# The order in which an instruction's waits are issued, in a kernel planned op by op

## The chip, the cores and the metric

The kernel runs on one core of a Trainium2 chip. The metric is the device time of one execution in microseconds (us), lower being better; times of several runs are given as their median. A profile of one execution is read beside them.

## The reference

Four layers follow each other on a sequence of 2048 rows of 512 numbers: A, B, A, B. Each normalizes its input and adds its result to it.

```python
# A: 32 query heads of 16, one key head and one value head for all of them
scores = jnp.einsum("bhqd,bkd->bhqk", q, k) * (Dh ** -0.5)
p = _softmax(scores, axis=-1)
o = jnp.einsum("bhqk,bkd->bhqd", p, v)
# B: linear attention, 32 heads of 16
phi = lambda t: jnp.where(t > 0, t + 1, jnp.exp(t)) + 1e-6
kv = jnp.einsum("bhsd,bhse->bhde", pk, v)
o = num / den
x = x + _A_ref(_layernorm(x, axis=-1), ...)   # then B, A, B
```

## The kernel before

Nothing is looped on the chip. Python code describes the work as operations, a planner in the same file runs them once against its own estimate of time, and the order that comes out on each engine is what is issued. The stretches that fill most of the time are the two A layers. There a group of two or three score blocks (128 keys by 512 columns, four heads by 128 queries) is made by TensorE into two or three PSUM banks (line 807, called from the operation of line 965). ScalarE takes the exponential of the whole group into one of six PT buffers (line 973). TensorE then multiplies PT by V into an accumulation bank (line 861). Beside this, VectorE makes a further block's exponential by integer arithmetic from PSUM into FB (line 1049), adds shifted copies of it (line 1080), and TensorE multiplies those too by weighted V (also line 861). Short matmuls of line 906 fill TensorE where it has nothing else. GpSimd computes the power of each layernorm (line 655). SyncE issues all DMAs (lines 507, 583, 1467).

An operation may be issued when those that it depends on are done: those that wrote what it reads, and those that wrote or read what it overwrites. `Planner.op` collects them in a Python set, `o.deps`. The planner notes for each operation the time at which it is planned to end, `o.end`. When the order of all engines is fixed, `finalize` (lines 274 to 294) gives each operation that others need a place in the count of its engine's semaphore (`s_pe`, `s_act`, `s_dve`, `s_pool`); a DMA gets one of 24 semaphores of its own.

`emit` (lines 296 to 313) then walks one engine's order. For each operation it keeps, of every engine that it depends on, the dependency with the highest count, in a dictionary `need`, whose order is the order in which the set gave them up: that of the objects in memory, not of time. A dependency on the same engine counts too on VectorE, ScalarE and GpSimd; so an exponential of line 973 waits for TensorE (`s_pe`: the scores, or the matmul that read the PT buffer last) and, if that is not covered by an earlier wait, for ScalarE itself (`s_act`: the exponential that wrote the same PT buffer some five exponentials earlier). A score matmul of line 807 waits for ScalarE and VectorE, which read its banks before. For each entry of `need` not already waited for, `eng.wait_ge` is called (line 310), and then the operation is issued.

## Time and profile before

| what | value |
| --- | --- |
| median of 3 runs | 1555.51 us (1555.47 to 1560.37) |
| the profiled execution: time | 1556.79 us |
| the profiled execution: span from first to last instruction | 1555.1 us |
| granted TensorE clock, mean | 0.996 |
| TensorE matmul, ScalarE, VectorE busy | 1458.7, 1476.8, 1448.3 us |
| GpSimd busy | 68.8 us |
| line 973, exponentials on ScalarE | 1361, 1424.5 us busy |
| line 807, score matmuls | 4096 |
| line 861, matmuls by V | 4068 from FB, 3079 from PT |

PE is TensorE's matmul, PEld its loading of weights, ACT ScalarE, DVE VectorE, POOL GpSimd, SP SyncE. A q behind an engine's name (ACTq) means its sequencer: the part that takes the instructions in order and hands them to the engine. In a group's line stand the source line, the engine, the operation, what is written and read with the sizes, how many there are, busy time and mean duration, and the idle time just before them with what ended most of it. The chain of work that ended last is followed back from the last instruction, at each step to what released it, or to the instruction before it on its engine; "issue" in it is time in which an engine waited for nothing that the profile shows.

### The profile page before, as it was taken

How to read it: one execution, taken by the hardware profiler on the slowest of the kernel's cores; microseconds unless marked ns; L12 is line 12 of the kernel's file. 1: busy time of each engine (PE TensorE's matmuls, PEld its weight loads, DVE VectorE, ACT ScalarE, POOL GpSimd, SP SyncE). 2: the span in 40 equal slices, each digit the busy share in tenths (PEclk: the TensorE clock that was granted, in tenths of full speed). 3: DMA queues.
4: the chain of work that ended last, by engine and by line, in shares of the span. 5: the costliest groups of instructions: out<-in, count | busy, mean ns of one | idle time of the engine just before them, and what ended most of it. 6: DMA issues, size and time to landing. Idle time of an engine off the chain costs nothing.

```text
span 1555.1 us, 36056 instructions
## 1 busy us (share of the span) xinstructions
PE 1458.7 (94%) x14602; PEld 535.4 (34%) x14713; DVE 1448.3 (93%) x2707; ACT 1476.8 (95%) x1500; POOL 68.8 (4%) x122
## 2 busy tenths in 40 slices
PE   8998999999999999999999989999999999999999
PEld 4322332333333333333644323323333333333345
DVE  7999999999999999998676799999999999999977
ACT  8999999999999999999699999899999999999982
POOL 4000000000000000000111000000000000000000
PEclk9999999999999999999999999999999999999998
DMA  5100010000000000000000000000000000000001
GB/s 132 47 2 1 8 22 5 8 8 5 8 8 8 5 8 5 1 1 1 2 1 1 1 1 15 15 8 8 6 9 5 8 8 8 5 5 2 1 2 55
DMA packets 40435, 17.55 MB, mean 11 GB/s; under 512 B 34128, under 2 KB 39760, under 8 KB 40272
## 3 DMA queue, kind: packets, MB, share of 16 engines
q1 hardware_dynamic: 40272, 15.25, 4.2%
q8 instruction: 118, 1.93, 0.5%
q14 instruction: 45, 0.37, 0.1%
HBM read 5.28 MB, written 2.10 MB: 5 GB/s over the span
## 4 chain that ended last, share of the span: by engine, by line
PE 32%; issue 23%; DVE 23%; ACT 20%; POOL 1%; DMA 0%; SPq 0%; ACTq 0%; POOLq 0%; DVEq 0%
ACT PT L973 19%; DVE FB L1049 11%; PE ps L861 11%; PE ps L807 9%; DVE FB L1080 6%; PE ps L575 4%; PE ps L906 2%; PE ps L732 2%; PE ps L1122 1%; POOL rs L655 1%; DVE st L651 1%; DVE sacc L1103 1%; PE ps L793 1%; ACT phE L1205 1%; DVE xn L658 1%
## 5 line engine op out<-in xcount | busy, mean ns | idle before, releaser
L973 ACT ACTIVATE PT<-ps 128x1024 bf16<-128x1024 f32 (+1 forms) x1361 | 1424.5, 1180 | 19.9 <-PE ps L861 13.4
L1049 DVE TENSOR_SCALAR FB<-ps 128x512 int16<-128x512 f32 x1017 | 675.0, 686 | 23.5 <-PE ps L807 20.7
L807 PE MATMUL ps<-QT,KM 32*128 32x512 bf16 x4096 | 533.4, 384 | 46.8 <-ACT PT L973 27.9
L861 PE MATMUL ps<-FB,VW 128*32 128x512 bf16 x4068 | 530.4, 385 | 19.5 <-ACT PT L973 9.5
L861 PE MATMUL ps<-PT,V 128*32 128x512 bf16 x3079 | 513.0, 386 | 9.7 <-ACT PT L973 5.6
L1080 DVE TENSOR_SCALAR FB<-FB 128x2048 int16<-128x2048 int16 (+1 forms) x765 | 503.0, 683 | 0.9
L807 PEld LDWEIGHTS ps<-QT,KM 32*128 32x128 bf16 x4096 | 139.8, 91 | 445.3 <-ACT PT L973 203.8
L861 PEld LDWEIGHTS ps<-FB,VW 128*32 128x32 bf16 x4068 | 133.4, 94 | 219.5 <-issue 113.0
L861 PEld LDWEIGHTS ps<-PT,V 128*32 128x32 bf16 x3079 | 125.9, 94 | 111.8 <-issue 56.1
L906 PE MATMUL ps<-QT,V 128*32 128x512 bf16 (+6 forms) x568 | 131.0, 315 | 0.9 <-DVE FB L1049 0.9
L655 POOL TENSOR_TENSOR rs<-ve,mhalf 128x1 f32<-128x1 f32 x64 | 51.7, 811 | 1398.9 <-DVE ve L653 1386.0
L575 PE MATMUL ps<-wqkv,xnT 128*128 128x512 bf16 (+1 forms) x211 | 65.1, 368 | 3.9 <-issue 2.9
L906 PEld LDWEIGHTS ps<-QT,V 128*32 128x32 bf16 x568 | 44.1, 95 | 59.6 <-issue 39.3
L1103 DVE COPY sacc<-ps 128x512 f32<-128x512 f32 x64 | 43.8, 684 | 7.8 <-PE ps L861 7.6
L1205 ACT ACTIVATE phE<-ps 128x512 bf16<-128x512 f32 (+1 forms) x66 | 41.3, 625 | 6.6 <-PE ps L732 4.7
L1122 PE MATMUL ps<-identF,sacc 128*128 128x128 f32 x256 | 45.9, 291 | 1.5 <-DVE sacc L1103 0.8
L732 PE MATMUL ps<-xnT,wqkv 128*128 128x128 bf16 x512 | 44.3, 221 | 0.0
L651 DVE BATCH_NORM_STATS2 st<-x_sb 128x6 f32<-128x512 bf16 x60 | 40.8, 683 | 2.6 <-DMA x_sb<-in_A_x_dram 2.3
L1105 DVE TENSOR_TENSOR sacc<-sacc,ps 128x512 f32<-128x512 f32 x56 | 38.2, 682 | 2.4 <-PE ps L861 2.1
L732 PE MATMUL ps<-xnT,wq 128*128 128x128 bf16 x480 | 38.6, 224 | 0.0
L575 PEld LDWEIGHTS ps<-wqkv,xnT 128*128 128x128 bf16 x272 | 21.8, 97 | 44.9 <-issue 34.2
L732 PEld LDWEIGHTS ps<-xnT,wqkv 128*128 128x128 bf16 x512 | 29.1, 98 | 22.8 <-issue 19.4
(115 smaller groups left out, 671.1 us busy)
## 6 DMA issues: line engine op xcount, KB each, us to landing
out_dram<-x_sb SPq DMA_DIRECT2D x16, 128.0 KB, 1.7
x_sb<-in_A_x_dram SPq DMA_DIRECT2D x3, 512.0 KB, 6.1
wqkv<-in_B_wqkv_dram SPq DMA_DIRECT2D x1, 1536.0 KB, 7.5
xnT<-xn SPq DMA_TRANSPOSE x36, 2.4
x_sb<-in_A_x_dram SPq DMA_DIRECT2D x4, 128.0 KB, 2.2
wq<-in_A_wq_dram SPq DMA_DIRECT2D x1, 512.0 KB, 4.2
wo<-in_A_wo_dram SPq DMA_DIRECT2D x1, 512.0 KB, 4.1
wo<-in_B_wo_dram SPq DMA_DIRECT2D x1, 512.0 KB, 8.5
```

Source lines behind the costliest of these rows:

```text
L575: return e.matmul(dst, lhsT=l, rhs=r, start=(k == 0), stop=(k == len(pairs) - 1))
L655: op({PO: (0.55, lambda e: e.tensor_tensor(out=rs[:, t:t + 1], in0=ve[:, t:t + 1], in1=mhalf[:], op=ALU.pow))}, reads=[("ve", t), "mhalf"] ...
L732: ins = e.matmul(dst[:, g * P:(g + 1) * P], lhsT=lhs(g, k), rhs=rhs(k), start=(k == 0), stop=(k == FT - 1))
L807: return e.matmul(bank(b), lhsT=KM[r, sg.par, kt * P:(kt + 1) * P], rhs=QT[r, sg.t, :], start=True, stop=True)
L861: ins = e.matmul(ps[32 * j:32 * j + 32, ACC * 512:(ACC + 1) * 512], lhsT=V[:, kt, :] if w is None else VW[:, kt, w, :], rhs=ap, start=(k = ...
L906: o = op({PE: (n / 2400.0, lambda e: e.matmul(ps[32 * j:32 * j + 32, b * 512:b * 512 + n], lhsT=V0[:], rhs=QT[:, sg.t, 0:n], start=st, sto ...
L973: ex = op({AC: (0.05 + 0.4267 * n, lambda e, n=n, s_=s_, p_=p_: e.activation(PT[:, p_, 0:n * 512], ps[:, s_ * 512:(s_ + n) * 512], ACTF.Ex ...
L1049: o = op({DV: (0.60, lambda e: e.tensor_scalar(out=dst.bitcast(I16), in0=bank(b), scalar1=VB, scalar2=VLO, op0=ALU.add, op1=ALU.max))}, wr ...
L1080: o = op({en: (du, lambda e, w=w, g_=g_: e.tensor_scalar(out=FB[:, g_, 0:n].bitcast(I16), in0=FB[:, f_, 0:n].bitcast(I16), scalar1=float(w ...
L1103: o = op({DV: (0.6, lambda e, src=src: e.tensor_copy(src, bank(ACC)))}, writes=[B_(ACC), key], prio=0.0, lat=0.15)
L1122: o = op({PE: (0.12, lambda e, c=c: e.transpose(ps[:, b * 512 + c * P:b * 512 + (c + 1) * P], src[:, c * P:(c + 1) * P], identF[:]))}, rea ...
L1205: op({AC: (0.07 + n / 1200.0, lambda e: e.activation(phE[:, i, 0:n], bank(b, n), ACTF.Exp))}, reads=[B_(b)], writes=[("phE", i)], prio=min ...
```

## The change

One line of `emit` changes. The entries of `need` are taken in the order of the planned ends of their operations, the earliest first. What is waited for, how often, and the order of the instructions on each engine stay as they are.

```diff
                 if k not in need or need[k].value < d.value:
                     need[k] = d
-            for k, d in need.items():
+            for k, d in sorted(need.items(), key=lambda x: x[1].end):
                 if waited.get(k, 0) >= d.value:
                     continue
                 waited[k] = d.value
                 eng.wait_ge(d.sem, d.value)
             ins = o.fn(eng)
```

## The prediction

> **What bounds the kernel now.** I read the page first: busy shares and the chain that ended last.

> ```profile
> span 1555.1 us, 36056 instructions
> PE 1458.7 (94%) x14602; PEld 535.4 (34%) x14713; DVE 1448.3 (93%) x2707; ACT 1476.8 (95%) x1500; POOL 68.8 (4%) x122
> ...
> PE 32%; issue 23%; DVE 23%; ACT 20%; POOL 1%; DMA 0%; SPq 0%; ACTq 0%; POOLq 0%; DVEq 0%
> ```

> Three engines are busy for 93 to 95% of the span, and none carries the chain: it changes hands between PE, DVE and ACT all the time. So no engine's throughput alone sets the end, and the delay of a handoff (semaphore counted up, next instruction starts) is paid wherever the chain crosses. Handoffs are all that this change touches.

> Next, the instructions of line 310, which are the waits that stand alone:

> ```profile
> L310 ACTq EVENT_SEMAPHORE  x1175: 17/17/1615, 6.3 to 1549.4; - x196
> L310 PEldq EVENT_SEMAPHORE  x875: 51/51/51, 5.5 to 1538.6; - x175
> L310 DVEq EVENT_SEMAPHORE  x114: 21/21/842, 23.0 to 1549.2; - x114
> L310 SPq EVENT_SEMAPHORE  x77: 17/17/26862, 173.8 to 1554.6; - x77
> L310 POOLq EVENT_SEMAPHORE  x52: 17/17/17, 214.6 to 1513.7; - x52
> ```

> Each is the second wait of a two-wait instruction (of SP, of one with up to four). Most are ACT's and PE's; DVE, at 2707 instructions, has only 114.

> Third, the chain in time order (start us, us, what) at single handoffs. PE to ACT at 1137, then at 775:

> ```profile
> 1137.56 0.35 PE ps L807 x3
> 1137.91 0.02 issue
> 1137.93 0.02 ACTq L310
> 1137.94 0.04 issue
> 1137.99 1.03 ACT PT L973
> ```

> ```profile
> 774.83 0.39 PE ps L807 x2
> 775.22 0.02 issue
> 775.24 0.02 ACT PT L973
> ```

> In the first the wait that ended last (on `s_pe`) stood in the EVENT_SEMAPHORE: 0.08 us pass. In the second the exponential carried it, the separate wait (on `s_act`) having been over long before: 0.02 us. ACT to PE at 180.9 and at 119.7 shows the same pair:

> ```profile
> 179.93 0.93 ACT PT L973
> 180.85 0.14 issue
> 180.99 0.39 PE ps L807 x3
> ```

> ```profile
> 118.55 1.19 ACT PT L973
> 119.74 0.05 issue
> 119.79 0.39 PE ps L807 x3
> ```

> 0.14 us against 0.05 us. So the trace of before holds both forms and prices them.

> **What the change does.** It adds, removes and moves no instruction; the order on every engine is the same. It only decides which of two waits an instruction carries. The words say "in the order of planned end", which sounds as if the last one stood next to the instruction. In the program built from the changed kernel it is the other way round: of the calls ahead of an operation, the first is the wait that the instruction carries, and the later ones stand in EVENT_SEMAPHOREs before it. For an exponential of line 973 the calls now come as `s_act` (an exponential some five back), then `s_pe` (the scores); built, the EVENT_SEMAPHORE holds `s_pe` and the exponential carries `s_act`. The wait planned to end last is thus always the separate one: the dear form throughout.

> In before the order is that of a set, hence mixed. I went through the trace's instruction records, which name the semaphore each waits for, and set them beside the times at which the semaphores counted up. Of line 973's 1361 exponentials 263 have one wait, 788 carry `s_pe` (cheap form) and 310 carry `s_act` (dear). After, all 1098 are dear. Over all instructions with two waits, cheap to dear go: ACT 826, PE 311, DVE 60, POOL 26. Dear to cheap, where plan and trace disagree on which wait ends last: PE 39, others none. The rest keep their form.

> **Prices,** from the last semaphore update to the start of the instruction, where it started at once:
> - ACT: 22 to 23 ns carried, 82 to 83 ns separate; 60 ns more.
> - PE: 41 to 42 ns to the first weight load carried, 104 ns separate. But the rest of the group then trickles out: from update to the update made by a group of three score matmuls it is 461 against 547 ns; 87 ns more.
> - DVE: 23 against 92 ns; 69 more. POOL: 68 against 133 ns; 65 more.
> - SP is not priced: it is 0% of the chain, its DMA transposes land in 2.4 us (median), and its issues keep their order. I take it as nothing; if that cover fails, each of 60 transposes would be late by what the other engines show, 0.06 to 0.09 us, of which the chain holds hardly any.

> Behind the separate wait stand the instruction itself and the rest of that engine's order. On ACT that is the next exponential; its PT then reaches the matmuls of line 861 late, and its banks reach the score matmuls of line 807 late. On PE the matmuls by V queue behind a late score group.

> [...]

> **The sum.** Most waits are over before their engine is free; only late ones pay. Two bounds:
> - Along the chain. Following each instruction back to the update that released it within 8 ns of the prices above, and otherwise to its predecessor, I find 422 handoffs. Of these 79 on ACT, 7 on PE, 5 on DVE, 4 on POOL go from cheap to dear, 1 on PE back: 79 x 60 + 6 x 87 + 5 x 69 + 4 x 65 = 5.9 us. With durations unchanged the end cannot come earlier than this same chain allows, so this is the floor of my forecast.
> - All of it. Wherever an instruction that flips would have to start later than it did: ACT 205 times, 10.5 us in all; PE 129 times, 5.8 us at 63 ns each at most, 8.0 at 87; DVE 1.2; POOL 1.6; less 12 x 87 ns = 1.0 where PE gains. Laid end to end, +20.3 us.

> The truth is near the floor, because the pushes off the chain fall in parallel with it: 126 of ACT's 205 and 122 of PE's 129 lie beside it. But a path that was only some tens of ns shorter comes level and counts. I add 1.1 us for that, some 8% of the 14.4 between the bounds, and take **+7.0 us**. Against the profiled execution's own 1556.8 us (span 1555.1 and 1.7 around it) that gives 1563.8; this execution lay 1.3 us over the median, so from the median 1555.5 I say **1562.5 us**, 0.45% slower. A measurement here can tell about 0.3%, 4.7 us, from no change.

> **Rivals.**
> - *Absorbed.* ACT is 95% busy, so only places where it stood idle pay: of the 788 cheap exponentials 45 had idle time before them, 45 x 60 ns = 2.7 us, the time 1558.2. Against it: exponentials of 1024 columns last 1.02 to 1.08 us but start 0.904 us apart when packed, so a late one shows no gap and is late all the same; 164 flips on ACT were already at the minimum of 22 ns.
> [...]
> - *The words come true*: the latest wait is carried. Then the chain's dear handoffs become cheap: ACT 52 x 60, PE 58 x 87, DVE 7 x 69, POOL 4 x 65 = 8.9 us at most; other paths would soon take over, so I take about half, 1551.5, faster. It decides if the exponentials of the changed kernel carry `s_pe`. The built program says that they carry `s_act`.
> - *Everything adds up*: the full 20.3 us, 1575.8, if each push on PE also delays the exponential behind it. For it speaks that the chain alternates; against it ACT's median of some 230 ns between update and start.

> **Chances.** Forecast 0.74, absorbed 0.12, reads ahead 0.03, words come true 0.04, everything adds up 0.07. The forecast's floor, 1561.4, is above the 1560.2 that 0.3% makes; I leave 0.01 of it under that. Slower by over 0.3%: 0.73 + 0.07 = 0.80; within 0.3%: 0.12 + 0.03 + 0.01 = 0.16; faster: 0.04. The range takes in the absorbed case and about two thirds of the way to the last, 1557.5 to 1571; some 0.12 stays outside.

> **What would show it.** EVENT_SEMAPHORE counts stay at 1175, 875, 114, 77 and 52, and durations stay. In the chain, PE to ACT reads 0.02 issue, 0.02 ACTq, 0.04 issue at every two-wait exponential, and ACTq and issue grow in its share. ACT's busy time stays near 1477 us while its span grows. The loss builds up in step with time through both A layers, since late exponentials are spread over them. I am wrong if exponentials carry `s_pe`, if the dear form is there and the span has not grown by 5 us, or if the loss sits in one place.

## The result

| kernel | median of runs | against before, 95% interval | last `zb` copy starts (profiled) |
| --- | --- | --- | --- |
| before | 1555.59 us (13 runs) | | 1518.8 us |
| changed | 1563.49 us (13 runs) | 1.0044 (1.0032 to 1.0056) | 1525.8 us |

0.44% of 1555.6 us are 6.8 us (5.0 to 8.7); the medians themselves differ by 7.9. The last column is the start of the last copy into the tile `zb`, line 1332, a mark near the end of the second A layer.

The page of the changed kernel, where the prediction showed before's:

```profile
span 1559.3 us, 36056 instructions
## 1 busy us (share of the span) xinstructions
PE 1458.6 (94%) x14602; PEld 536.4 (34%) x14713; DVE 1451.4 (93%) x2707; ACT 1480.3 (95%) x1500; POOL 66.8 (4%) x122
...
PE 36%; DVE 31%; ACT 24%; issue 7%; POOL 1%; DMA 0%; SPq 0%; ACTq 0%; DVEq 0%; POOLq 0%
```

Instructions, and busy time to a few us, are the same; the EVENT_SEMAPHOREs are 1175, 875, 114, 77 and 52 as before. The two largest groups of them in the changed kernel:

```profile
L310 ACTq EVENT_SEMAPHORE  x1175: 17/17/38, 7.8 to 1553.6; - x196
L310 PEldq EVENT_SEMAPHORE  x875: 51/51/51, 5.5 to 1543.2; - x175
```

So the time is neither in new instructions nor in longer ones.

Where it is, the table by windows tells. The borders are 40 us, the start of the first `zb` copy, a point 68 us behind it at which both kernels have done nearly the same matmuls, and the start of the last `zb` copy. Before, then after (window, its length, busy us and instructions of PE, PEld, DVE, ACT and POOL, granted clock, DMA share, GB/s):

```profile
40.00:747.00 707.00, 667.09 (x6683) 228.02 (x6727) 683.22 (x1227) 693.03 (x700) 17.31 (x16) 1.00 0.03 8
747.00:815.00 68.00, 64.84 (x684) 32.92 (x686) 49.02 (x124) 60.03 (x65) 8.08 (x17) 1.00 0.01 1
815.00:1518.80 703.80, 662.01 (x6604) 235.35 (x6657) 658.58 (x1208) 684.00 (x684) 23.87 (x31) 1.00 0.03 6
1518.80:1555.10 36.30, 32.65 (x292) 20.59 (x294) 27.20 (x48) 7.34 (x13) 0.00 (x0) 0.86 0.18 59
```

```profile
40.00:749.90 709.90, 668.83 (x6679) 229.48 (x6722) 684.37 (x1226) 694.26 (x699) 15.95 (x16) 1.00 0.03 7
749.90:818.00 68.10, 64.59 (x682) 32.89 (x684) 48.71 (x122) 59.88 (x65) 8.09 (x17) 1.00 0.01 1
818.00:1525.80 707.80, 664.16 (x6608) 237.05 (x6660) 660.54 (x1210) 686.03 (x685) 23.26 (x31) 1.00 0.03 6
1525.80:1559.30 33.50, 29.88 (x292) 19.12 (x294) 27.11 (x48) 7.33 (x13) 0.00 (x0) 0.94 0.19 64
```

The A layers lose 2.9 and 4.0 us, the stretch between them 0.1: 7.0 together. That is a little too small, since 40 us is a fixed time: up to it the changed kernel was granted a clock of 1.00 against 0.96 and had done 353 matmuls against 349. From the start of ScalarE's 46th instruction (44.3 us before, 43.6 after) to the last `zb` copy it loses 7.7 us, 3.6 of them up to the first copy. The last stretch is 2.8 us shorter in this one execution, whose TensorE was granted 0.94 of its clock there against 0.86; that is why the two spans differ by 4.2 us only.

One handoff shows the cause: the chain at the exponential that the prediction showed at 775.24, with 0.02 us of issue between update and start. In the changed kernel:

```profile
777.98 0.39 PE ps L807 x2
778.36 0.02 issue
778.38 0.02 ACTq L310
778.40 0.04 issue
778.45 0.17 ACT PT L973
```

The wait for the scores now stands in the EVENT_SEMAPHORE, and 0.08 us pass.

### The profile page after: what moved, and what is told of

It reads as the page before. It is cut to its first block, busy times and chain, and to the rows that moved or that the text cites. A ratio compares the mean times of both kernels' runs of the same rounds, so it can differ in the third digit from the quotient of the medians.

```text
span 1559.3 us, 36056 instructions
## 1 busy us (share of the span) xinstructions
PE 1458.6 (94%) x14602; PEld 536.4 (34%) x14713; DVE 1451.4 (93%) x2707; ACT 1480.3 (95%) x1500; POOL 66.8 (4%) x122
## 4 chain that ended last, share of the span: by engine, by line
PE 36%; DVE 31%; ACT 24%; issue 7%; POOL 1%; DMA 0%; SPq 0%; ACTq 0%; DVEq 0%; POOLq 0%
ACT PT L973 23%; DVE FB L1049 15%; PE ps L861 13%; PE ps L807 11%; DVE FB L1080 9%; PE ps L575 4%; PE ps L906 2%; PE ps L732 2%; PE ps L1122 2%; ACT phE L1205 1%; DVE sacc L1103 1%; DVE st L651 1%; PE ps L793 1%; POOL rs L655 1%; DVE sacc L1105 1%
## 5 line engine op out<-in xcount | busy, mean ns | idle before, releaser
L973 ACT ACTIVATE PT<-ps 128x1024 bf16<-128x1024 f32 (+1 forms) x1361 | 1427.8, 1175 | 23.0 <-PE ps L861 15.5
L807 PE MATMUL ps<-QT,KM 32*128 32x512 bf16 x4096 | 533.2, 383 | 51.9 <-ACT PT L973 27.9
L807 PEld LDWEIGHTS ps<-QT,KM 32*128 32x128 bf16 x4096 | 142.8, 90 | 451.9 <-ACT PT L973 154.1
L732 PE MATMUL ps<-xnT,wqkv 128*128 128x128 bf16 x512 | 44.3, 221 | 0.0
```

The costliest lines, as they stand in the source:

```text
L732: ins = e.matmul(dst[:, g * P:(g + 1) * P], lhsT=lhs(g, k), rhs=rhs(k), start=(k == 0), stop=(k == FT - 1))
L807: return e.matmul(bank(b), lhsT=KM[r, sg.par, kt * P:(kt + 1) * P], rhs=QT[r, sg.t, :], start=True, stop=True)
L973: ex = op({AC: (0.05 + 0.4267 * n, lambda e, n=n, s_=s_, p_=p_: e.activation(PT[:, p_, 0:n * 512], ps[:, s_ * 512:(s_ + n) * 512], ACTF.Ex ...
```

## The experiments

Theory: a wait that ends late costs more when it stands apart in an EVENT_SEMAPHORE than when the instruction carries it, and the changed kernel puts the latest wait apart everywhere. Rivals: any order fixed in time is worse than before's mixture; the loss comes from the clock that the runs were granted; every EVENT_SEMAPHORE costs, wherever it stands. Each kernel was timed beside before on the same chip, e1 to e4 on one and e5 to e7 on another; before's median was 1556.4 us on the first and 1556.3 on the second.

The mark near the end also holds what the clock did at the start: over the first 40 us the profiled executions were granted between 0.91 (e2) and 1.00 (e4, changed). The last column of the table leaves that out. It is the time from the start of ScalarE's 46th instruction, at 43 to 46 us, to the last `zb` copy, less the same in e1; the clock is 1.00 there in all of them. Before stands at 4.0 in it, the changed kernel at 11.7.

| kernel | median | against before, 95% interval | last `zb` copy | to it from ACT's 46th, over e1 |
| --- | --- | --- | --- | --- |
| e1, late wait carried everywhere | 1552.44 us | 0.9977 (0.9962 to 0.9991) | 1515.4 us | 0 us |
| e2, apart on ACT alone | 1558.18 | 1.0014 (1.0005 to 1.0023) | 1523.1 | 6.3 |
| e3, apart on PE alone | 1556.36 | 0.9998 (0.9989 to 1.0006) | 1518.9 | 3.5 |
| e4, implied waits left out | 1551.18 | 0.9967 (0.9955 to 0.9979) | 1515.3 | 0.0 |
| e5, apart on DVE, POOL, SP alone | 1554.00 | 0.9987 (0.9975 to 0.9999) | 1515.6 | 0.9 |
| e6, late wait apart twice on ACT | 1576.93 | 1.0133 (1.0113 to 1.0153) | 1541.0 | 24.8 |
| e7, early wait apart twice on ACT | 1551.93 | 0.9966 (0.9953 to 0.9978) | 1514.2 | -0.1 |

**e1: the order turned round.**

```diff
-            for k, d in sorted(need.items(), key=lambda x: x[1].end):
+            for k, d in sorted(need.items(), key=lambda x: x[1].end, reverse=True):
```

> The changed kernel with the order of the calls turned round on all engines: the wait planned to end last is called first, so that the instruction itself carries it, and earlier ones stand in EVENT_SEMAPHOREs. Theory (a late wait costs 60 ns more on ACT and 87 ns more on a PE score group when it stands apart): faster than before, by no more than the 8.9 us that before's chain holds in dear handoffs, and by about 2 to 4 us, since other paths come level: 1552 to 1554 us; exponentials start 22 ns after the last update. Rival 1 (any fixed order in time costs, since the mixed one was better): slower than before, like the changed kernel, 1562 to 1564. Rival 2 (the form does not matter, the 7 us come from the clock that the runs were granted): the same time as the changed kernel at the same clock.

Measured: 1552.44 us, 4.0 under the before timed beside it. That is the theory's number; the first two rivals fall. On the clock: the profiled e1 was granted 0.996 of it over its span, as before was, and its span is 1551.4 us against 1555.1. The runs at 0.996 took 1553.1 to 1553.3 us in e1 and 1562.3 and 1563.5 in the changed kernel. The same handoff in e1:

```profile
773.00 0.39 PE ps L807 x2
773.38 0.02 issue
773.40 0.02 ACT PT L973
```

The instructions, their order and the number of waits are those of the changed kernel, which is 10.4 us slower by the ratios (1.0044 less 0.9977).

**e2 and e3: one engine at a time.** The comments, which name the run, are not in the kernels.

```diff
-            for k, d in sorted(need.items(), key=lambda x: x[1].end):
+            for k, d in sorted(need.items(), key=lambda x: x[1].end, reverse=(e != AC)):   # e2
+            for k, d in sorted(need.items(), key=lambda x: x[1].end, reverse=(e != PE)):   # e3
```

> As e1, but on ACT alone the wait planned to end last stands apart (1098 exponentials, as in the changed kernel). Theory: before's chain has 79 + 52 = 131 late two-wait handoffs on ACT, 131 x 60 ns = 7.9 us is the most that this can add to e1; I expect 4 to 7 us more than e1. Rival (PE, with the dearer price of 87 ns, carries most of the loss): less than 2 us more than e1.

> As e1, but on PE alone the wait planned to end last stands apart. Theory: before's chain has 7 + 58 = 65 late two-wait handoffs on PE, 65 x 87 ns = 5.7 us at most; PE stands ready earlier than its matmuls are needed in most places, so 1 to 4 us more than e1, and less than ACT's share in e2. Rival: as much as e2 or more, 5 us and up.

Measured: e2 is 5.7 us over e1, e3 3.9 (by the medians; 5.8 and 3.3 by the ratios). Both lie where the theory put them, ACT above PE. The mark of line 1332 (what follows "to" is the start of the last copy), e1, e2, e3:

```profile
L1332 DVE TENSOR_TENSOR zb<-ps,mask x4: 158/174/193, 745.3 to 1515.4; 128x24 bf16<-128x24 f32 x2, 128x8 bf16<-128x8 f32 x2
```

```profile
L1332 DVE TENSOR_TENSOR zb<-ps,mask x4: 158/176/191, 749.5 to 1523.1; 128x24 bf16<-128x24 f32 x2, 128x8 bf16<-128x8 f32 x2
```

```profile
L1332 DVE TENSOR_TENSOR zb<-ps,mask x4: 158/176/194, 747.4 to 1518.9; 128x24 bf16<-128x24 f32 x2, 128x8 bf16<-128x8 f32 x2
```

At the first copy e2 is 4.2 us behind e1 and e3 2.1, at the last one 7.7 and 3.5. Of e2's, 1.4 us were there already at ScalarE's 46th instruction, behind the start at 0.91 of the clock; without them it is 2.8 and 6.3. So each loss builds up along both A layers.

**e5: the other three engines.** The condition is `reverse=(e in (AC, PE))`.

> As e1, but on DVE, POOL and SP the wait planned to end last stands apart, on ACT and PE it is carried. Theory: before's chain has 12 late two-wait handoffs on DVE and 8 on POOL, 12 x 69 + 8 x 65 ns = 1.3 us; SP, which the prediction took as nothing, adds nothing: 0 to 2 us more than e1. With e2's 5.7 and e3's 3.9 this should make up what the changed kernel has over e1 (about 11 us). Rival (SP's DMA issues or POOL's short handoffs, unpriced or thinly priced, matter): 3 us and more over e1.

Measured: 1.6 us over e1 by the medians, 0.9 from ScalarE's 46th instruction to the last `zb` copy; the intervals of e1 and e5 overlap. It is small, as expected, and the rival, 3 us and more, falls. The three parts, 5.7 + 3.9 + 1.6 = 11.2 us, make up the distance of the changed kernel from e1 (10.4 by the ratios); in the last column of the table they are 6.3 + 3.5 + 0.9 = 10.7 of 11.7.

**e4: without needless waits.** A wait is left out where one that the engine has already made implies it. `d.knows` holds all that had been waited for when `d` ran, by its engine and by those it waited for; the method that fills it is not shown.

```diff
+            for k, d in sorted(need.items(), key=lambda x: x[1].end, reverse=True):
                 if waited.get(k, 0) >= d.value:
                     continue
                 waited[k] = d.value
+                for j, v in d.knows.items():
+                    waited[j] = max(waited.get(j, 0), v)
                 eng.wait_ge(d.sem, d.value)
```

> As e1, but a wait is left out where another wait of the same engine already implies it (an exponential that waits for the matmuls that read a PT buffer need not wait for the exponential that wrote it). EVENT_SEMAPHOREs fall from 1175 to 0 on ACT, from 114 to 18 on DVE, from 52 to 0 on POOL, and stay at 870 on PE. Theory (a separate wait that is over early costs nothing, only where the late one stands matters): the time of e1 within 2 us. Rival (every EVENT_SEMAPHORE costs its engine time, 17 ns on ACT by its own record): 1175 x 17 ns = 20 us less than e1 if all of it lay on the path, 5 us or more less if a quarter did.

Measured: 1.3 us under e1, and the same at the last `zb` copy (1515.3 against 1515.4; 0.0 in the last column). ACT has lost all its 1175 separate waits and gained nothing that the A layers show. The rival falls. Its median is the lowest measured and beats both kernels, though e1, e4 and e7 cannot be told apart by their intervals.

**e7 and e6: one more separate wait,** on ACT, for operations with two waits; e7 on e1, e6 on the changed kernel. `mine`, 0 at the start of each operation, counts its waits; `d` is what the loop called last: the earlier wait in e7, the later one in e6. With two more calls the built program has two EVENT_SEMAPHOREs in place of one, the second holding the wait twice.

```diff
                 eng.wait_ge(d.sem, d.value)
+                mine += 1
+            if e == AC and mine > 1:
+                for _ in range(2):
+                    eng.wait_ge(d.sem, d.value)
```

> As e1, but on ACT each operation with two waits gets two EVENT_SEMAPHOREs in place of one, both for the earlier wait; the late one is carried. Theory (a separate wait that is long over costs nothing, as the sequencer passes it while the engine works): the time of e1 within 1.5 us. Rival (each EVENT_SEMAPHORE costs its engine time): 1175 x 17 ns = 20 us more if all lay on the path, over 3 us in any case.

> The changed kernel, but on ACT each operation with two waits gets two EVENT_SEMAPHOREs in place of one, both for the wait planned to end last. Theory (the price is the time that the sequencer needs from the update through the separate instruction to the next): an exponential released late starts later by at least the 17 ns that such an instruction lasts and by up to some 45 ns, so around 100 to 130 ns after the update instead of 82; on the changed kernel's 179 late ACT handoffs 3 to 8 us more than the changed kernel. Rival (the price comes from the engine's queue having run dry, however many instructions stand there): the changed kernel's time within 1.5 us.

Measured: e7, with 1175 more EVENT_SEMAPHOREs than e1, takes 0.5 us less by the medians (1.7 by the ratios), and the intervals overlap; in the last column of the table the two differ by 0.1 us. The rival falls a second time: a separate wait that is over costs nothing here. e6 is 13.4 us over the changed kernel (13.1 in the last column), where 3 to 8 were expected. The direction holds and the rival falls; the size does not hold. The same handoff, in e6 (its lines are 5 further down):

```profile
786.49 0.39 PE ps L812 x2
786.88 0.02 issue
786.90 0.02 ACTq L315
786.91 0.04 issue
786.95 0.04 ACTq L315
786.99 0.04 issue
787.04 0.17 ACT PT L978
```

In the records of e6 the first EVENT_SEMAPHORE starts 22 ns after the update, the second at 77, the exponential at 160. An instruction recorded with 17 ns thus holds the next one back by 55, and the second, recorded with 38, by 83. So the record can be much shorter than the step, 17 ns of 55. The wait can be in it all the same: five of before's on SyncE, with two waits each, are recorded with 1.1 to 26.9 us and end 22 to 23 ns after the update that they waited for. I had taken the record for nearly the whole step: 17 to 45 ns. With 160 - 83 = 77 ns on the 179 late ACT handoffs of the changed kernel's chain the sum is 13.8 us, against 13.4 measured.

## Why the prediction was right, and where it was not

- **The total** was right: +7.0 us forecast, 6.8 measured (5.0 to 8.7), and 7.7 from ScalarE's 46th instruction to the last `zb` copy. The floor along the chain, 5.9, held; the added 1.1 for paths that come level was an estimate and is not shown by itself, so that the total came within 0.2 us is in part luck.
- **Where it builds up** was right: 3.6 us of the 7.7 come up to the first `zb` copy and 4.1 behind it.
- **The build turns the order round**: shown. The exponential of the fence at 778.45 waits behind an EVENT_SEMAPHORE, and in the records of the changed kernel all 1098 exponentials with two waits carry `s_act`. e1, whose calls come the other way, is the fast one.
- **The prices** stayed, in the changed kernel's trace: ACT 83 to 84 ns apart, 23 carried; PE 105 and 42, its group of three score matmuls 547 and 461 to the update; DVE 93, POOL 133.
- **The words come true** was priced at 1551.5; e1, which is that case, took 1552.4. That before's dear handoffs give only about half of their 8.9 us back was a guess, and 4.0 came back.
- **Absorbed** was rightly put low, and the reason can be seen. The group of exponentials before and after:

```profile
L973 ACT ACTIVATE PT<-ps 128x1024 bf16<-128x1024 f32 (+1 forms) x1361 | 1424.5, 1180 | 19.9 <-PE ps L861 13.4
L973 ACT ACTIVATE PT<-ps 128x1024 bf16<-128x1024 f32 (+1 forms) x1361 | 1427.8, 1175 | 23.0 <-PE ps L861 15.5
```

  The first line is before's. The idle time grew from 19.9 to 23.0 us, 3.1 and no more. ACT's busy time grew by 3.5, from 1476.8 to 1480.3, though the single exponential lasts no longer (1175 ns against 1180). Packed exponentials overlap in the records: those of 1024 columns last 1.02 to 1.08 us, and the most frequent distance between two starts is 0.904 us. Before has 515 starts 904 or 905 ns behind the one ahead, the changed kernel 474. Pulled apart they cover more time. The prediction saw the overlap but still said that busy time would stay near 1477; that step was wrong.
- **Reads ahead**, 0.03 among the chances, stands for the case that both forms cost the same and the time stays. No run shows them at one price. At 245 places on ACT in e2, most of them exponentials, the instruction started 77 to 87 ns after the update of the later wait, which stood apart, and none earlier; in e1, where it is carried, 225 started at 22 to 32.
- **Issue and ACTq grow in the chain's share**: wrong. Issue fell from 23% to 7% on the page, and in e1, the faster kernel, it is 66%. The share is made of a few places where the view finds no releaser. One such piece of before, in the chain in order of time:

```profile
866.14 93.19 issue
```

  93 us in one piece, in which PE, DVE and ACT are busy for 85, 88 and 91 us. Single handoffs in the chain can be read; that share cannot be compared between kernels.
- **The profiled execution** was forecast at 1563.8 us and took 1560.97: the clock of its last stretch, above, and of its first 40 us. The median was forecast at 1562.5 and came to 1563.49. One of the prediction's own signs of being wrong, a span that has not grown by 5 us, is there in this execution (4.2 us): the sign took no account of the clock.

Open: what SP, POOL and DVE share of e5's 0.9 to 1.6 us; and whether a two-wait EVENT_SEMAPHORE (38 ns recorded) is dearer than a second one with one wait would be, since e6 had no such form.

## What to carry to other kernels

Where an instruction has several waits, see in the built program which of them it carries itself: the one that ends last belongs there, and the separate ones should be long over. Here that alone decides between 1552.4 and 1563.5 us, with the same instructions in the same order. A sort that sounds right in the source can come out reversed behind the builder; leaving out waits that others imply removes the question on an engine, as on ACT in e4. Before's mixture is that of objects in memory, so another build of the same source can carry other waits: its 1555.6 us belong to this mixture.

## What the runs showed of the hardware beyond that

The granted TensorE clock differed between single runs of the changed kernel, and the time with it: 1560.82 us at 0.999, 1563.49 at 0.996, 1568.24 at 0.992. That spread is as large as the effect under study. Comparing one execution with one other, at an unequal clock, would have given 4.2 us for 6.8. Stretches that ran at a clock of 1.00 in both, taken between the same two instructions, gave 7.7; they also show e4 and e7 within 0.1 us of e1, where the medians differ by 1.3 and 0.5.
